# A new hand-out of engines and turn numbers for a two-layer linear-attention and gated-MLP kernel

## The chip, the cores and the metric

The kernel runs on one core of one Trainium2 chip. A core has five engines that run their own instruction streams and meet only at semaphores: TensorE (PE: matmuls, with its weight loads shown apart as PEld), VectorE (DVE), ScalarE (ACT), GpSimd (POOL) and SyncE (SP, which here only issues DMAs). The metric is the device time of one execution in microseconds. Before the change it is 391.01 us, the median of 3 runs (390.86 to 391.19).

## The reference

Input x has 2048 rows of 512 in bf16. Two blocks A and B are applied in turn, twice, each on the layer-normed x and added to x:

```python
x = x + A(layernorm(x)); x = x + B(layernorm(x))      # layer 0
x = x + A(layernorm(x)); x = x + B(layernorm(x))      # layer 1, same weights

# A: linear attention, H = 32 heads of Dh = 16, no mask
q, k, v = split(x @ wqkv)
phi(u)  = concat(softmax(u @ w_phi), softmax(-(u @ w_phi)))    # 32 features a head
kv = phi(k)^T v;  z = sum over rows of phi(k)
o  = (phi(q) kv) / (phi(q) z + 1e-6);  A = o @ wo

# B: gated MLP, F = 1376
B = (relu(x @ W_gate) * (x @ W_up)) @ W_down
```

`kv` and `z` are sums over all 2048 rows, so no query of a layer can be answered before the last key of that layer is in.

## The kernel before

**Tiling.** The rows are 16 tiles of 128, in five slabs of 2, 4, 4, 4 and 2 tiles (`SLABS`). All of x stays on chip. `w_phi` is folded into the key and query weights at the start (`fold`: transposes `wtr`, evictions `wtcp`, products `wcomp`, evictions `wccp`). For every slab and layer there are stages, each with a tag: layer norm (`la`, `lg`), keys and values (`k`), queries (`q`), sums of the query softmax (`z`, `at`), spreading of the denominators (`sp`), numerators (`nm`), output projection (`wo`), gate and up products (`gx`, `gl`) and the down projection (`d`). `gl13` is layer 1, slab 3.

**Layer norm and its transpose.** DVE takes statistics (L844, L869), ACT the root (L871, L873), DVE, ACT or POOL applies it (`ytile`, L886 or L889). The result must be transposed before TensorE can use it: for most slabs by a DMA with transpose that SP issues, one a tile (`ytx`, L894), for the others by TensorE (L918, and the evictions at L817/L820).

**Keys** (`keys`, from L929). A tile has four matmuls for k and four for v (L706), two exponentials of k on ACT (`expk`, L946), their group sums (`Zk`, L952, DVE, 128x1024 to 128x64), the reciprocals (`rZk`: L955 on DVE, or a logarithm and an exponential on ACT, L958 and L959), an eviction of v (`vsb`, L817 on DVE or L820 on ACT), and two products v times 1/Z (`vhat`, L966, on POOL or DVE). Then come the key-value products (`kv`, L978): 32 matmuls of 34 columns a tile, issued for two tiles at a time in slabs of four. They are the shortest matmuls of the kernel.

**An alternative for `Zk`** exists in the code (`sums_by_pe`): two transposing DMAs of `expk` from SP, then eight matmuls of 8 columns on TensorE. The kernel before uses it for no tile.

**Queries** (`queries`, `attend`, from L1037): matmuls with `Wqp`, exponentials on ACT, then sums by short matmuls (`zz`, `zd`, L1062; `za`, L1075), some of which travel through DRAM and back (`zao`, `zai`). Denominators are spread over partitions for slabs 0 and 1 by TensorE (L1184) and multiplied in by DVE (L1202, or after a copy by ACT at L1199), for the other slabs by DMAs (`aTo`, `abT`) and a multiplication on DVE or POOL (L1169). Numerators are L1136, their eviction `oT`.

**The MLP** (`rest`, `glu`) is most of TensorE's work: long runs of 256- and 512-column matmuls (L706), a ReLU on ACT (L1258), a product on DVE (L1260), the down projection and its residual on DVE (L1206).

**What sets the order.** Nothing is ordered by hand. The program makes a list of 3220 operations, each bound to an engine. `ENG` is a dictionary that overrides the default engine of single operations: the key `vh/0/12/1` is the second `vhat` product of tile 12 in layer 0, `vc` an eviction of v, `rz` a reciprocal, `es` and `em` multiplications by the spread denominators, `ap` the application of a layer norm, `yc` the eviction of a transpose, `ot` that of a numerator, `za` that of the sums, `ft` and `fc` evictions of the fold, `ms` memsets and masks, `ld` a load, and `zk` the way in which `Zk` is made. `TURNS` gives each operation a number, in the order in which the program creates them. `schedule()` walks through the list with a small model of the core: of the operations that can start first on an engine, the one with the lowest number goes. The order that comes out, engine by engine, is what the chip executes; each engine is strictly in order and waits on semaphores. The model's constants have no other effect on the program. One part of the model concerns instruction loading: TensorE's stream is cut into pieces of `CHUNK` instructions (two a matmul; the first piece has `CHUNK0`), and a piece may not be entered sooner than `FETCH` nanoseconds after the one before it.

**Fillers.** 18 matmuls with no use of their results (`filler`, L790) carry the number 99999 and run where TensorE would idle early in the program.

In `emit`, an operation that waits on two semaphores gets a separate wait instruction for one of them:

```python
for s, c in self.waits[o.idx]:
    if isinstance(s, int):
        eng.wait_ge(dsems[s], 16 * c)
    else:
        eng.wait_ge(sems[s], c)
ins = o.fn(eng)
```

Of the kernel before, what the change touches and what calls it, by code (L numbers as in the profile page):

```python
# [32 lines left out]
 'ap/a11/2': 'pool',  # L33
 'ap/a11/3': 'act',
 'ap/a12/0': 'act',
 'ap/a12/1': 'pool',
 'ap/a12/2': 'act',
# [3 lines left out]
 'ap/g01/3': 'act',  # L41
# [3 lines left out]
 'ap/g03/1': 'act',  # L45
 'ap/g11/0': 'act',
 'ap/g12/0': 'act',
 'ap/g12/3': 'act',
 'ap/g13/0': 'act',
 'ap/g14/0': 'act',  # L50
# [6 lines left out]
 'em/10/03': 'dve',  # L57
 'em/11/02': 'act',
 'em/11/03': 'dve',
 'es/02/0': 'pool',  # L60
 'es/02/1': 'pool',
 'es/02/3': 'pool',
# [3 lines left out]
 'es/12/1': 'pool',  # L66
 'es/13/0': 'pool',
 'es/13/2': 'pool',
 'es/13/3': 'pool',
 'es/14/2': 'pool',  # L70
 'fck1': 'act',
 'fck3': 'act',
 'fcq2': 'dve',
 'ftk3': 'act',
 'ld/wphi': 'sp',
 'ld/x0': 'act',
 'ms/ZD 0': 'pool',
 'ms/kvs 0 1': 'pool',
 'ms/kvs eps 0': 'pool',
 'ot/00/0': 'dve',  # L80
 'ot/00/1': 'act',
 'ot/00/3': 'act',
 'ot/01/3': 'dve',
 'ot/02/0': 'dve',
 'ot/02/1': 'dve',
 'ot/02/2': 'dve',
 'ot/02/3': 'dve',
 'ot/03/0': 'dve',
 'ot/04/2': 'dve',
 'ot/10/2': 'dve',  # L90
 'ot/11/0': 'dve',
 'ot/11/2': 'dve',
 'ot/12/2': 'dve',
 'ot/13/0': 'dve',
 'ot/14/1': 'dve',
 'ot/14/2': 'dve',
 'ot/14/3': 'dve',
 'rz/0/1': 'act',
 'rz/0/13': 'act',
# [6 lines left out]
 'rz/0/9': 'act',  # L106
 'rz/1/0': 'act',
 'rz/1/10': 'act',
 'rz/1/13': 'act',
 'rz/1/15': 'act',  # L110
 'rz/1/4': 'act',
 'rz/1/6': 'act',
 'rz/1/7': 'act',
 'rz/1/8': 'act',
 'vc/0/2': 'dve',
 'vc/0/5': 'dve',
 'vc/0/6': 'dve',
 'vc/0/7': 'dve',
 'vc/0/8': 'dve',
 'vc/0/9': 'dve',  # L120
 'vc/1/10': 'dve',
 'vc/1/11': 'dve',
 'vc/1/12': 'dve',
 'vc/1/14': 'dve',
 'vc/1/2': 'dve',
 'vc/1/4': 'dve',
 'vc/1/6': 'dve',
 'vc/1/9': 'dve',
 'vh/0/12/1': 'dve',
# [5 lines left out]
 'vh/0/2/0': 'dve',  # L135
 'vh/0/4/1': 'dve',
 'vh/0/7/1': 'dve',
 'vh/0/8/1': 'dve',
 'vh/0/9/1': 'dve',
 'vh/1/1/0': 'dve',  # L140
 'vh/1/1/1': 'dve',
 'vh/1/13/1': 'dve',
 'vh/1/14/1': 'dve',
 'vh/1/15/0': 'dve',
 'vh/1/15/1': 'dve',
 'vh/1/3/0': 'dve',
 'vh/1/3/1': 'dve',
 'vh/1/6/1': 'dve',
 'xp/a02': 'pe',
# [3 lines left out]
 'yc/a00/1': 'dve',  # L153
# [13 lines left out]
 'yc/g00/0': 'dve',  # L167
# [12 lines left out]
 'za/02': 'dve',  # L180
 'za/11': 'dve',
 'za/12': 'dve'}
# [7 lines left out]
-29 100 315 38 249 -1 -5 378 124 183 441 1025 890 766 504 639 1282 1154 1343 1406 1595 1469 1532 1217 1091 1917 150 -100 169 96 147 0 235 48 49 22 51  # L190
70 113 155 198 244 284 326 380 99999 99999 99999 99999 99999 99999 99999 99999 99 84 64 175 296 389 413 -83 467 471 478 484 584 765 770 776 782 825
369 377 433 423 459 724 717 738 744 779 659 665 671 676 701 880 886 891 897 967 544 560 571 572 635 858 863 869 874 903 99999 99999 99999 99999 99999
99999 99999 99999 99999 99999 247 374 -117 444 476 247 589 616 622 628 683 311 393 422 323 492 549 555 577 583 649 799 1078 1099 1271 934 970 1035
1056 1494 1398 1651 1884 1158 1931 2050 828 1143 1164 1183 948 992 1013 1121 1350 1254 1470 1684 2279 1209 2300 2418 3183 3208 3287 1450 1482 1596
1623 1700 1362 1366 1378 1373 1494 1307 1318 1324 1324 1406 1290 1302 1302 1307 1444 595 752 537 653 694 817 759 858 888 957 989 1036 1023 996 1043
1086 1214 1380 1341 1307 1300 1606 1629 1672 1686 1650 1886 1928 1954 1778 1878 1948 2338 2415 2055 3024 2525 1553 1723 1749 1769 1461 1574 1780 1864
1817 1923 2209 2469 2183 2733 2626 1430 1488 1510 1531 1847 1915 1965 2003 1685 1540 2540 2699 2229 2838 3080 1807 2106 2152 2191 2482 2527 2527 2565
2503 2700 2738 2988 3257 2631 3295 3401 3135 4011 4098 924 1029 866 982 1075 1575 1133 1641 1684 1739 1943 1936 1938 2032 2108 1965 2171 2253 2430
2361 2396 2337 2706 2798 2846 2956 2970 3078 3103 3237 3028 3092 3177 3478 3515 3413 3749 3643 2496 2818 2867 2898 2621 2677 2735 2742 3209 3000 3320
3468 3498 2861 3537 3864 2784 3011 3013 3257 3284 3303 3298 3368 3369 3321 3547 3832 3479 4110 3918 2905 2930 3036 3068 3347 3390 3411 3433 3273 3417  # L200
3714 3903 3968 3655 4096 4636 3961 4756 4917 1191 1935 1191 1763 1844 2490 1765 2333 2671 2790 2836 2980 2864 3144 2946 3265 3003 3384 3078 3671 3692
3735 3757 3584 3578 3627 3649 3807 3863 3990 4133 3919 4202 4308 3541 3563 3843 3930 3714 3800 3822 4265 3984 4032 4175 4301 4346 4634 4418 4113 4203
4201 4200 4286 4360 4589 4630 4275 4250 4469 4595 4646 4733 5017 3455 3476 3779 3908 3498 3519 4277 4394 4115 4141 4361 4722 4803 4722 4950 4952 4706
5131 5276 2125 2621 2689 2802 2848 3156 3527 1583 2330 2400 2481 2686 2732 2817 4437 4459 4481 4502 3865 3902 4524 4837 4552 4600 4700 4832 4879 4886
5144 5080 4070 4092 4221 4308 4632 4653 4675 4924 4394 4442 4809 4941 5150 5006 5143 5268 5326 5326 5408 137 224 153 5458 5501 5512 5537 5502 2301
2314 2334 2347 2343 2383 2378 2381 3627 3536 2035 2033 2046 2049 2132 2189 2205 2216 2447 2583 5106 5262 5546 5604 5653 5673 5705 5743 5811 5954 5878
6014 5895 5974 6167 6334 6388 6438 6516 6491 6509 6504 6637 6723 6788 6834 6915 6464 6522 6658 6680 6702 6783 6863 6915 6968 7001 7035 7112 7118 7123
7129 7162 6957 7136 7023 7065 7134 7140 7146 7151 7195 2581 2601 2642 2696 2809 2846 1815 2059 2097 2133 2357 2292 4203 4329 4416 4945 5102 5054 2412
2413 2430 2454 3579 2542 5181 5283 5567 5651 5696 5740 5761 5857 5976 6047 6107 6066 6380 6426 6509 6142 6470 6260 6318 6323 6591 6659 6728 6776 6659
6766 6831 6874 6918 6968 6853 6939 6982 7069 7290 6745 6961 7004 7090 7230 6810 6868 7026 7004 7091 7350 7589 7524 7604 7408 7582 7466 7597 7715 7782  # L210
7828 7821 7814 7980 7911 8225 7842 8260 8066 8391 7925 7218 7268 7234 7243 7678 7686 8051 8061 8114 8199 8522 7273 7612 7623 7634 7645 7656 7667 7694
7749 7771 7792 7847 7913 7924 7934 7945 7734 7985 7339 7350 7361 7372 7437 7459 7481 7579 7382 7393 7404 7421 7426 7448 7424 7503 7619 7691 7306 7317
7507 7514 7546 7557 7568 7601 7251 7262 7284 7295 7309 7525 7535 7590 8246 8316 7814 7825 7858 7869 7902 7956 7967 7978 7836 7918 7989 8000 8011 8022
8033 8033 8065 8139 8067 8076 8085 8097 8113 8118 8143 8143 7705 7716 7727 7738 7760 7730 7803 7880 8186 8251 8223 8267 8288 8310 8443 8464 8486 8507
8529 8989 9027 9185 8159 8180 8202 8245 8387 8421 8551 8572 8594 8615 8861 8972 9294 9361 9069 9279 9391 9488 9703 9346 9504 9696 9878 10465 10583
10630 10312 11431 11603 12580 12497 10420 10374 10876 10785 10937 12732 13713 12996 14406 14363 14453 14005 10745 10692 11539 11598 14372 14119 14410
14577 11401 14635 14749 20550 20652 20690 4816 4880 5323 5302 5409 5361 4373 4545 4567 4902 5313 4958 4859 4988 5010 5075 5214 5166 4967 5025 5404
5420 5527 5479 5722 5857 5883 6201 6560 6607 6631 6707 6750 6867 6804 7141 7078 7267 7330 7393 7456 7519 7204 7427 7641 8078 7855 8335 8541 8422 8422
8481 8788 8840 8883 8904 9026 9331 9309 9339 9431 9672 8637 8659 8680 8767 8817 10932 11123 10044 10404 10269 9127 9286 9616 9657 8892 9245 9879 11100
10730 11380 10496 10716 10726 10909 10680 10785 10798 11640 11092 10558 11494 8926 8934 8943 8951 8959 9003 9063 9104 9144 9252 8831 9191 9215 9175  # L220
9273 9229 9249 9258 9294 9347 9516 10615 10694 10724 10344 9728 9884 9905 9932 10391 10431 9287 9309 9436 9419 9040 9062 9122 9143 9748 9626 9100 9165
9186 9682 9595 9669 9725 9752 9563 9842 8723 8745 8810 9005 9600 9612 9753 9661 11274 11079 9880 10035 9979 10166 9394 9591 9868 10038 10348 10188
9729 9758 9857 9855 8702 9266 9395 9482 9947 10093 10485 10581 10583 10048 10793 10640 10808 10634 11222 11277 10219 9887 10004 9791 10025 10743 10219
10329 10254 10209 10560 10386 10511 10533 9903 9924 9958 10014 10420 10596 10711 10543 10819 10580 11313 10896 10995 10986 11256 11514 11009 11093
11568 12067 11334 11599 11437 11840 11521 11567 11313 11744 11114 10837 11512 11754 11926 11802 11929 12325 12024 11758 12492 12484 10520 11062 10784
# [87 lines left out]
FUSEZ = ()  # L313
ZALL = ()
LATE = 300.0
TRUNC = 0
LASTCUT = ((0, 256), (256, 512))
# [51 lines left out]
class Program:  # L369
# [4 lines left out]
    DMA_BW = 345.0  # L374
    SWITCH = 95.0
    RING = 5500.0
    CHUNK, CHUNK0 = 256, 193
    FETCH, FETCH0 = 3700.0, 9000.0

    def __init__(self):  # L380
# [1008 lines left out]
```

## Time and profile before

| what | value |
|---|---|
| median of 3 runs | 391.01 us (390.86 to 391.19) |
| the profiled execution's own time | 390.13 us |
| its span, first to last instruction | 388.4 us |
| granted TensorE clock | 1.000 |
| PE busy | 376.3 us (97%), 3785 matmuls and as many weight loads |
| DVE busy | 276.0 us (71%), 563 instructions |
| ACT busy | 191.9 us (49%), 428 instructions |
| POOL busy | 75.7 us (19%), 68 instructions |
| instruction loading of one queue | 30 packets, 0.49 MB |

TensorE's busy time counts matmuls that overlap in its pipeline: a 512-column matmul is shown with 379 ns, but the next one starts about 216 ns after it. So what matters is the distance between starts, and the places where a start is late. The chain of work that ended last is followed back from the end; "issue" in it is time in which the engine waited for nothing that the profile shows. Who ended a wait is inferred from the semaphores' events close to the wait's end.

### The profile page before, as it was taken

The numbers are of one execution on the slowest core, as the hardware profiler recorded it, in microseconds if no ns is written. First come the engines' busy times: TensorE is split into PE (matmuls) and PEld (weight loads), VectorE is DVE, ScalarE is ACT, GpSimd is POOL, SyncE is SP. The second block draws the span as 40 slices with busy tenths as digits, with TensorE's granted clock in tenths as the row PEclk, the third lists the DMA queues.
The fourth block names the chain that finished last, engine by engine and source line by source line (L and its number), as shares of the span: only waits on it lengthen the run. The fifth ranks groups of instructions, "written<-read, shape, count | busy, mean of one in ns | idle before, by whom it ended". The sixth has DMA issues, their size and how long they took to land.

```text
span 388.4 us, 9066 instructions
## 1 busy us (share of the span) xinstructions
PE 376.3 (97%) x3785; PEld 198.1 (51%) x3785; DVE 276.0 (71%) x563; ACT 191.9 (49%) x428; POOL 75.7 (19%) x68
## 2 busy tenths in 40 slices
PE   7999998999999999999999989999999999999996
PEld 4554454574444544444566545466444454544564
DVE  8999988977765667664797888788764567345343
ACT  6999689560453524242534478973353134224211
POOL 1065730060200500020223653003002410000000
PEclk9999999999999999999999999999999999999999
DMA  7995001144504212121003010213534132112002
GB/s 241 241 369 101 9 3 56 53 133 83 137 19 97 54 27 54 16 41 28 15 2 62 2 30 3 84 38 113 110 84 127 30 96 55 30 27 54 15 27 63
DMA packets 56970, 27.46 MB, mean 71 GB/s; under 512 B 39296, under 2 KB 55264, under 8 KB 56928
## 3 DMA queue, kind: packets, MB, share of 16 engines
q1 hardware_dynamic: 56352, 26.37, 26.6%
q8 instruction: 30, 0.49, 0.6%
q10 hardware_dynamic: 576, 0.49, 0.4%
q14 instruction: 12, 0.10, 0.1%
HBM read 14.73 MB, written 4.00 MB: 48 GB/s over the span
## 4 chain that ended last, share of the span: by engine, by line
PE 83%; DVE 11%; DMA 4%; issue 1%; ACT 0%; DVEq 0%
PE pb L706 78%; DVE stats L844 3%; DMA yG<-ytile 2%; PE pb L978 2%; DVE Zk L952 2%; DVE expq L1202 1%; DMA yA<-ytile 1%; PE pb L1136 1%; DMA x_sb<-in_A_x_dram 1%; PE pb L1075 1%; DVE yA L817 1%; DVE ytile L889 1%; PE pb L1062 1%; DVE vsb L817 0%; DVE mv L869 0%
## 5 line engine op out<-in xcount | busy, mean ns | idle before, releaser
L706 PE MATMUL pb<-yG,Wg 128*128 128x512 bf16 (+1 forms) x400 | 97.1, 337 | 0.0
L1258 ACT ACTIVATE gate_sb<-pb 128x512 bf16<-128x512 f32 x80 | 47.1, 596 | 99.0 <-PE pb L706 75.1
L706 PE MATMUL pb<-Wd,hT 128*128 128x512 bf16 (+4 forms) x363 | 95.4, 373 | 0.0
L706 PE MATMUL pb<-yG,Wu 128*128 128x512 bf16 (+1 forms) x400 | 91.8, 336 | 0.0
L1260 DVE TENSOR_TENSOR hT<-gate_sb,pb 128x512 bf16<-128x512 bf16 x80 | 54.0, 684 | 47.1 <-PE pb L706 29.4
L1206 DVE TENSOR_TENSOR x_sb<-x_sb,pb 128x512 bf16<-128x512 bf16 x59 | 39.3, 682 | 32.7 <-PE pb L706 32.4
L706 PEld LDWEIGHTS pb<-yG,Wg 128*128 128x128 bf16 x400 | 38.8, 98 | 32.4 <-issue 0.6
L706 PEld LDWEIGHTS pb<-yG,Wu 128*128 128x128 bf16 x400 | 38.8, 98 | 31.0 <-DVE x_sb L1206 0.4
L706 PEld LDWEIGHTS pb<-Wd,hT 128*128 128x128 bf16 (+1 forms) x363 | 34.9, 98 | 35.4 <-issue 0.6
L966 POOL TENSOR_TENSOR vhat<-vsb,rZk 128x544 bf16<-128x544 bf16 x31 | 33.5, 1101 | 55.7 <-DVE rZk L955 18.6
L1169 POOL TENSOR_TENSOR expq<-expq,abT 128x1024 bf16<-128x1024 bf16 (+1 forms) x11 | 20.7, 1899 | 118.1 <-DMA abT<-spread 61.6
L844 DVE BATCH_NORM_STATS2 stats<-x_sb 128x6 f32<-128x512 bf16 x60 | 39.5, 684 | 0.5 <-DMA x_sb<-in_A_x_dram 0.2
L706 PE MATMUL pb<-wv,yA 128*128 128x512 bf16 x128 | 38.0, 379 | 1.5 <-issue 1.5
L706 PE MATMUL pb<-Wkp,yA 128*128 128x512 bf16 x128 | 37.6, 379 | 1.0 <-DMA yA<-ytile 0.8
L706 PE MATMUL pb<-yA,Wqp 128*128 128x512 bf16 (+1 forms) x160 | 34.5, 338 | 0.9 <-DVE Zk L952 0.7
L1047 ACT ACTIVATE expq<-pb 128x512 bf16<-128x512 f32 x64 | 34.4, 613 | 1.7 <-PE pb L706 1.5
L706 PE MATMUL pb<-wo_sb,oT 128*128 128x512 bf16 x128 | 34.6, 379 | 0.0
L946 ACT ACTIVATE expk<-pb 128x512 bf16<-128x512 f32 x40 | 21.9, 612 | 10.0 <-PE pb L706 8.8
L952 DVE TENSOR_REDUCE Zk<-expk 128x64 f32<-128x1024 bf16 x20 | 24.2, 1209 | 1.4 <-ACT expk L946 1.2
L706 PEld LDWEIGHTS pb<-yA,Wqp 128*128 128x128 bf16 x160 | 14.6, 98 | 14.6 <-issue 1.9
L886 ACT ACTIVATE ytile<-x_sb,nmr,rstd 128x512 bf16<-128x512 bf16 x27 | 20.9, 807 | 0.5 <-DVE nmr L878 0.4
L706 PEld LDWEIGHTS pb<-Wkp,yA 128*128 128x128 bf16 x128 | 12.2, 98 | 15.9 <-issue 1.8
(106 smaller groups left out, 374.5 us busy)
## 6 DMA issues: line engine op xcount, KB each, us to landing
abT<-spread SPq DMA_DIRECT2D x32, 128.0 KB
out_dram<-x_sb SPq DMA_DIRECT2D x15, 128.0 KB, 1.8
x_sb<-in_A_x_dram SPq DMA_DIRECT2D x3, 512.0 KB
Wu<-in_B_W_up_dram SPq DMA_DIRECT2D x1, 1280.0 KB, 8.7
Wd<-in_B_W_down_dram SPq DMA_DIRECT2D x1, 1280.0 KB
Wg<-in_B_W_gate_dram SPq DMA_DIRECT2D x1, 1280.0 KB
sums_scr<-abT SPq DMA_DIRECT2D x5, 256.0 KB, 2.7
Zs<-sums_scr SPq DMA_DIRECT2D x5, 256.0 KB, 2.7
```

What stands on the lines that cost most here:

```text
L706: op("pe", lambda e: e.matmul(view(ps), lhsT, rhs, start=start, stop=stop), reads=reads, writes=[ps], occ=max(25.0, 0.4167 * n + 2.6), lat ...
L844: op("dve", lambda e: e.bn_stats(stats[:, t, :], src()), reads=[res], writes=[R("st", t)], occ=580, lat=680, name=f"bn{t}")
L886: op("act", (lambda t, yb: lambda e: e.activation(ytile[:, yb, :], x_sb[:, t, :], ACT.Identity, bias=nmr[:, t, :], scale=rstd[:, t, :]))(t ...
L946: op("act", (lambda i, s, pk: lambda e: e.activation(expk(i)[:, s, :], full(pk), ACT.Exp, scale=1.0 - 2.0 * s))(i, s, pk), reads=[pk], wri ...
L952: op("dve", (lambda i, zb: lambda e: e.tensor_reduce(Zk[:, zb, :], expk(i).rearrange("p s (h f) -> p (s h) f", f=16), AX.X, ALU.add))(i, z ...
L966: op(eng, (lambda i, s, vb, rz: lambda e: e.tensor_tensor(vhat(i)[:, s], vsb[:, vb, :, :], rZk[:, rz, s * 32:(s + 1) * 32].unsqueeze(2).to ...
L978: ins = e.matmul(ps.f32()[32 * i:32 * i + 32, g * 34:g * 34 + 34], expk(tiles[j])[:, sg, f0:f0 + 32], vhat(tiles[j])[:, sg, 8 * c + 2 * i: ...
L1047: op("act", (lambda c0, s, ps: lambda e: e.activation(eqv(st)[:, c0:c0 + per, s, :], ps.f32()[:, 0:per * n].rearrange("p (c n) -> p c n", ...
L1169: op(eng, lambda e: e.tensor_tensor(part, part, abT[:, c].rearrange("p (s n) -> p s n", s=2)[:, :, 0:n], ALU.mult), reads=Re + [R("abT", c ...
L1206: op("dve", lambda e: e.tensor_tensor(x_sb[:, t, :], x_sb[:, t, :], full(ps), ALU.add), reads=[R("x", t), ps], writes=[R("x", t)], occ=597 ...
L1258: op("act", (lambda gb, pg, k: lambda e: e.activation(gate_sb[:, gb, 0:k], pg.f32()[:, 0:k], ACT.Relu))(gb, pg, k), reads=[pg], writes=[R( ...
L1260: op("dve", (lambda gb, hb, pu, k: lambda e: e.tensor_tensor(hT[:, hb, 0:k], gate_sb[:, gb, 0:k], pu.f32()[:, 0:k], ALU.mult))(gb, hb, pu, k),
```

## The change

Three things are replaced and nothing else in the code:

- `TURNS` has 3222 new numbers in place of 3220.
- `ENG` differs in 101 keys. By kind, with what moves:
  - `vhat` (`vh`): 20 products come to DVE and 10 leave it; POOL has 10 fewer.
  - evictions of v (`vc`): 10 leave DVE for ACT, 3 come to DVE.
  - reciprocals (`rz`): 4 leave ACT for DVE, 3 the other way.
  - `zk/9` is new: the sums of tile 9 in layer 0 go by `sums_by_pe`, so DVE loses one `Zk`, SP gets two transposing DMAs and TensorE eight matmuls.
  - layer norm applications (`ap`): 6 come to ACT and 6 leave it; one moves between DVE and POOL each way.
  - `oT` evictions (`ot`): 7 come to DVE and 7 leave it; `za/03` comes to DVE; `em/10/03` goes to ACT with one more eviction.
  - `es`: 5 come to POOL, 5 leave it. Fold: `ftk2`, `fck2` come to DVE; `BD` goes to POOL. `yc/a00/1` and `yc/g00/0` leave DVE. A few memsets change places. `ld/x0` goes from the ACT queue to SP's.
- Of the model's constants, `CHUNK` is 253.6 in place of 256 and `LOADLATE` 150 and 200 ns in place of 100 and 150. `LATE=300` is the value that it had.

Since the numbers set the order, the whole order is new. The key-value products show it. Their turn numbers, first and second group of a slab:

| products | before | after |
|---|---|---|
| layer 0, slab 1 | 3135, 4011 | 3525, 3575 |
| layer 0, slab 2 | 3961, 4756 | 4322, 4801 |
| layer 0, slab 3 | 4706, 5131 | 4877, 5226 |
| layer 1, slab 0 | 20550, 20652 | 19364, 19436 |
| layer 1, slab 1 | 21691, 21741 | 19386, 19811 |
| layer 1, slab 2 | 21791, 22801 | 22019, 22716 |
| layer 1, slab 3 | 22851, 23191 | 22766, 23137 |
| layer 1, slab 4 | 23241, 23288 | 23379, 23426 |

Other numbers that the text below uses: the two DMAs of `zk/9` have 3619 and 3750 and its matmuls 4023; the transposes by DMA of slab 3, layer 0 (`la03`, tiles 12, 11, 13, 10) have 3095, 3226, 3357 and 3488, those of slab 4 (`la04`) 3881 and 4012.

```diff
 ENG = {...
- 'ld/x0': 'act',
+ 'fck2': 'dve',
+ 'ftk2': 'dve',
+ 'ms/BD': 'pool',
+ 'ot/00/2': 'dve',
+ 'za/03': 'dve',
- 'em/10/03': 'dve',
- 'vc/0/6': 'dve',
- 'vc/0/7': 'dve',
+ 'vc/0/11': 'dve',
- 'vc/0/9': 'dve',
+ 'vh/0/10/0': 'dve',
+ 'vh/0/11/0': 'dve',
+ 'vh/0/12/0': 'dve',
- 'vh/0/12/1': 'dve',
...
+ 'zk/9': 'pe'}
 TURNS = """
--29 100 315 38 249 -1 -5 378 124 183 441 1025 890 766 504 639 1282 1154 1343 1406 1595 1469 1532 1217 1091 1917 150
...
+63 50 315 0 252 126 0 441 189 378 504 960 829 698 567 1023 1924 2210 1798 2273 1280 1217 1861 1355 1154 1735 100
...
-ZALL=((0,2),(0,3),(0,4),(1,1),(1,2),(1,3),(1,4)); LASTCUT=((0,384),(384,512)); FILL=(8,10); LOADLATE=(100,150)
+ZALL=((0,2),(0,3),(0,4),(1,1),(1,2),(1,3),(1,4)); LASTCUT=((0,384),(384,512)); FILL=(8,10); LATE=300; LOADLATE=(150,200)
...
-    CHUNK, CHUNK0 = 256, 193
+    CHUNK, CHUNK0 = 253.6, 193
```

## The prediction

> **What bounds the kernel now.** The page first: TensorE is busy 97% of the span, and the chain that ended last lies on it for 83%.
>
> ```profile
> PE 376.3 (97%) x3785; PEld 198.1 (51%) x3785; DVE 276.0 (71%) x563; ACT 191.9 (49%) x428; POOL 75.7 (19%) x68
> PE 83%; DVE 11%; DMA 4%; issue 1%; ACT 0%; DVEq 0%
> q8 instruction: 30, 0.49, 0.6%
> ```
>
> The matmuls themselves change by eight, so the time can move only where a matmul starts late. The waits of TensorE name these places:
>
> ```profile
> PE pb L706 <- issue: 1.5, 1, 1.5
> PE pb L706 <- DMA yG<-ytile: 1.5, 2, 0.8
> PE pb L706 <- DMA yA<-ytile: 0.8, 1, 0.8
> PE pb L706 <- DVE Zk L952: 0.7, 1, 0.7
> PE pb L1062 <- issue: 0.6, 1, 0.6
> ```
>
> Then the timeline of PE around three of them (start, length, what, idle time before it and its releaser):
>
> ```profile
> 43.77 1.24 PE L706 MATMUL pb<-Wkp,yA 128*128 128x512 bf16 x5
> 45.74 0.39 PE L706 MATMUL pb<-yA,Wqp 128*128 128x512 bf16 x1 [0.73 <-DVE Zk L952]
> ...
> 223.66 0.38 PE L706 MATMUL pb<-Wkp,yA 128*128 128x512 bf16 x1
> 225.51 0.38 PE L706 MATMUL pb<-wv,yA 128*128 128x512 bf16 x1 [1.47 <-issue]
> ...
> 241.40 0.38 PE L1062 MATMUL pb<-expq,ZD 128*32 128x64 bf16 x26
> 242.34 0.23 PE L1062 MATMUL pb<-expq,ZD 128*32 128x64 bf16 x6 [0.56 <-issue]
> ```
>
> The third stall cuts one operation of 32 matmuls in two, where no semaphore stands: the instructions were not there. Counted in the trace (weight loads, matmuls and TensorE's separate waits), the last instruction before each gap is number 1217, 4801 and 5569, which is 193 + 256 times 4, 18 and 21. So all three stand at ends of pieces of 256 instructions; 0.49 MB in 30 packets is 16 KB a packet for 7,639 instructions, 255 each. The name that the profile gives to the first (DVE Zk) is then only what happened to end close by: in the program that matmul waits on DVE for kvsum (L988), which ended at 44.14. TensorE had crossed into the piece before at 42.42, 222.02 and 238.88 and goes on at 45.74, 225.51 and 242.34: a piece comes no sooner than 3.3 to 3.5 us after the last crossing. In these stretches 256 instructions were used up sooner, since the key-value products (L978) need about 9 ns a matmul against 216 for a 512-column one; ahead of 223 stand 192 of them in a row. Measured from start to start, less a normal distance, the stalls cost 0.90, 1.63 and 0.74: 3.3 us.
>
> The other places are transposes by DMA that the chain shows to be long:
>
> ```profile
> 32.73 4.47 DMA yA<-ytile
> ...
> 85.96 4.84 DMA yG<-ytile
> ...
> 274.79 3.67 DMA yG<-ytile
> ```
>
> From issue to landing such a transpose takes 2.5 us at the median (this line's answer: 2.4/2.5/4.3). TensorE stood 1.0, 0.87 and 0.92 us for these three. In each, a packet of an instruction queue was being moved (at 35.1, 86.3 and 275.8). Smaller waits are on DVE: about 1.6 us in all at 62.9 to 67.8, where VectorE multiplies spread denominators, and 0.35 at 255.4. The first 9 us are loads and warming.
>
> **The change part by part.** The profiled execution took 390.13 us with its span of 388.4; the median of the runs is 391.01, 0.9 above. I count on the span and put the difference on the median.
>
> *Key-value runs are pulled apart: -3.3 us.* In the old order layer 1's slab 1 (both groups) and the first group of slab 2 have neighbouring numbers (21691, 21741, 21791): the 192 matmuls. In the new one they are 19386, 19811 and 22019, with long matmuls between. In layer 0, 3961 and 4011 (128 matmuls) become 4322 and 3575. The sums that were cut at 242 have moved behind eight more query matmuls. Walking along the sorted new numbers with 193 + 256 n, less as many separate waits as the trace has up to there and with the fillers used in the first 16 us, and pricing by the trace (216 ns, 110 ns, 9 ns), the closest two crossings are 3.8 us apart (between the second group of slab 3 and `zd` of layer 0), the next 4.1 to 4.2 (layer 1, slab 3). Both are above 3.5, so no stall is left: from both sides 0 and -3.3. If the count is off by some 30 instructions, the sums `zd` of layer 1 come 2.8 us after the crossing before: 0.7 is lost again. I take -3.3.
>
> *`zk/9` by TensorE: +0.5.* Eight matmuls; a 128x128 product (`wcomp`) starts 56 ns after the one before, a weight load is 98: 0.45 to 0.8 us, all on the path. Zk's 1.21 us on DVE are saved beside it. The two DMAs occupy SP 1.27 us each, between slab 3's last transpose and slab 4's two, which wait behind them; the wait of the eight matmuls holds every matmul that follows, k and v of slabs 3 and 4. From the DMA number 3750 to 4023, and from 3881 to 4204 (first use of tile 14), about 2.7 to 3.2 us are left against 2.5 needed, so I take no wait; the lost cover is a rival below.
>
> *Late transposes: 0.* The new order again has its shortest leads in the same three places (2.9 to 3.3 us for a transpose of `la03`, `lg01` and `lg11`), each within 2 us of a crossing, and a new one in `la13`. Bounds: -2.8 if all three come free, +1.8 for two new ones at 0.9.
>
> *VectorE's order in the three stages that follow it: +1.3.* At the start `ftk2` and `fck2` (0.31 and 0.60 by neighbouring rows) come into DVE's queue before the layer norms; `BD` (0.59) and a copy (0.33) leave it; but tile 0's load goes second on SP, 0.45 after the first. The chain lies on DVE from 3.9 to 32.7, so I take +0.5 (between -0.5 and +1.5). At 62 to 68 a 256-column `oT` (0.42) and a 512-column copy `za/03` (0.69) join the queue that TensorE waits for: 0 to +1.1, I take +0.4. At 250, `em/10/03` gives DVE 0.26 us back but adds a link over ACT (0.60): -0.3 to +1.0, I take +0.4.
>
> *Hidden.* Engines stay under TensorE:
>
> ```profile
> L966 POOL TENSOR_TENSOR vhat<-vsb,rZk 128x544 bf16<-128x544 bf16 x31 | 33.5, 1101 | 55.7 <-DVE rZk L955 18.6 <-DVE mv L869 17.8 <-ACT rZk L959 8.5
> L966 DVE TENSOR_TENSOR vhat<-vsb,rZk 128x544 bf16<-128x544 bf16 x9 | 6.7, 777 | 0.0
> L817 DVE CAST vsb<-pb 128x512 bf16<-128x512 f32 x14 | 9.5, 684 | 4.1 <-PE pb L706 4.1
> ```
>
> Ten `vhat` cost DVE +7.8 and POOL -11; seven v evictions move 4.8 from DVE to ACT (604 ns each there); with Zk and one more reciprocal (0.55) DVE gains about 2 us in 276. Moves that even out (`ot`, `ap`, `es`) are nothing while those products run under the MLP's matmuls; uncovered, each costs its row, 0.4 to 0.8 us. The model's constants never reach the chip.
>
> Sum: -3.3 + 0.5 + 0 + 1.3 = -1.5 on 388.4: a span of 386.9, and 391.0 - 1.5 = **389.5 us**.
>
> [...]
>
> **Rivals.**
> - *The stalls are only moved.* The count of separate waits and fillers ahead of a place decides where a piece ends, and it is new. Against it: 3.8 us where 3.5 are needed. For it: that is thin, and three places are near. With one to three stalls of 0.7 to 1.6 back: 390.4 to 391.5. The change would then not do what it is said to do.
> - *The three gaps are not loading.* They belong to whatever else ends there (DVE, as the profile says of one), and stay: 391.0 + 1.8 = 392.8. Against it: three of three at the same rest of 256. [...]
> - *SyncE's queue at 34 to 44 us: slower.* Slab 3's transposes, `zk/9`'s two and slab 4's stand in one row, 1.27 us each, with a crossing near 36. A transpose as long as the chain's 4.5 us delays the sums of tile 9 and the transposes behind them; TensorE, in order, stands up to 1 us each for slab 3, the eight matmuls, and slab 4: +3, so 392.5. It decides if more than 2.3 us are lost there (391.8). For it: 1.0 is lost for slab 3 now, without the extra two.
> - *Fewer late transposes.* If two of the three come free, 389.5 - 1.8 = 387.7.
>
> **How the numbers follow.** A measurement can tell about 0.2% (0.8 us) from no change: faster is under 390.2, slower above 391.8. Forecast 0.55 (its own range 388.4 to 390.5, from the small terms); stalls moved 0.17; not loading 0.06; SyncE's queue 0.12; fewer late transposes 0.10. Faster: 0.50 + 0.03 + 0.09 = 0.62; slower: 0.01 + 0.02 + 0.06 + 0.11 = 0.20; same 0.18. The range from 387.7 to 392.3 leaves out the lower half of the last case and the upper parts of the third and fourth.
>
> **What the profile after would show.** No idle time of PE with "issue" over 0.3 us after the first 10 us, and none inside an operation; the word Zk gone from PE's waits. Starts late by 0.7 us or more for yA and yG, three of them. At 40 us eight short matmuls with little idle before them; if more than 0.5, the SyncE rival. 62 to 68 with 1.6 to 2.1 us idle. DVE 277 to 279, POOL 64 to 66 us busy. Gaps that cut a run at 193 + 256 n would make the first term wrong; new waits on DVE or ACT above 1 us elsewhere would make the sum wrong.

## The result, and the profile after

The changed kernel took 388.64 us (median of six runs, 388.32 to 389.36) against 390.94 beside it: a ratio of 0.9938, 95% interval 0.9921 to 0.9956. Forecast were 389.5 against 391.0, a ratio of 0.996, and a range of 387.7 to 392.3. The profiled execution took 388.32 us with a span of 386.5: 1.9 less span than before, where 1.5 were forecast. The size came out nearly as forecast; the working below it did not. The page of the changed kernel:

```profile
PE 371.2 (96%) x3743; PEld 197.6 (51%) x3793; DVE 277.8 (72%) x566; ACT 196.1 (51%) x433; POOL 66.5 (17%) x59
PE 86%; ACT 5%; DVE 3%; DMA 2%; issue 2%; SPq 1%; DVEq 0%; ACTq 0%
q8 instruction: 30, 0.49, 0.6%
```

(PE has 50 matmul records fewer than weight loads: those are missing in the trace, so starts are read from the weight loads below.) TensorE still carries the chain. Its waits (in total, times, longest), lines of the changed kernel being three higher:

```profile
PE pb L709 <- issue: 3.9, 16, 1.5
PE pb L709 <- ACT vsb L823: 0.8, 2, 0.6
PE pb L709 <- ACT oT L823: 0.5, 1, 0.5
PE pb L709 <- DVE stats L847: 0.2, 1, 0.2
```

The names Zk, yA and yG are gone from the long waits, and the gap inside L1062 (now L1065) is gone. But one wait of 1.5 us on "issue" stands there again. The chain of waits shows its place (start, length, what):

```profile
25.07 0.61 PE pb L981 x64
...
28.38 0.71 PE pb L709 x4
29.09 1.48 issue
30.57 8.15 PE pb L709 x38
...
44.01 0.24 issue
44.24 0.34 PE pb L1007 x8
...
87.65 3.22 DMA yG<-ytile
```

The 1.48 us stand between two query products of one group, 256 instructions behind the piece's end at 25.1 (instruction 193 + 512). Measured from weight load to weight load, less the normal distance, it costs 1.65. The eight matmuls of `zk/9` are the L1007 line: 0.34 us, with a late start before them.

Where TensorE lost time, in us, from the starts of all weight loads less normal distances:

| place | before | after |
|---|---|---|
| start of the kernel up to 20 us, the first matmul's later start with it | 3.5 | 4.1 |
| ends of pieces: 44.4, 223.7, 241.6 before; 28.8 after | 1.11 + 1.63 + 0.77 | 1.65 |
| late transposes: slab 3, layer 0; 90 us; 277 us | 1.18 + 1.08 + 1.13 | 0 + 0.31 + 0.84 |
| before the eight matmuls of `zk/9` | - | 0.58 |
| 62 to 75 us | 2.42 | 2.16 |
| 240 to 260 us, the stall at 241.6 set apart | 2.15 | 2.67 |

Two numbers about the ruler, since the effects are below 1%. In the three later groups of runs (the experiments) the kernel before had 389.2 to 389.5 us, with single executions from 387.8 to 392.5; and the changed kernel, run in the second of them once more as `e6_after_again`, gave 0.9981 [0.9960, 1.0002]. So the change is worth 0.2 to 0.6%, depending on the group, and the later interval just includes no change.

### The profile page after: what moved, and what is told of

The parts are those of the page before. It is cut to its first block, busy times and chain, and to the rows that moved or that the text cites. A ratio compares the mean times of both kernels' runs of the same rounds, so it can differ in the third digit from the quotient of the medians.

```text
span 386.5 us, 9068 instructions
## 1 busy us (share of the span) xinstructions
PE 371.2 (96%) x3743; PEld 197.6 (51%) x3793; DVE 277.8 (72%) x566; ACT 196.1 (51%) x433; POOL 66.5 (17%) x59
## 4 chain that ended last, share of the span: by engine, by line
PE 86%; ACT 5%; DVE 3%; DMA 2%; issue 2%; SPq 1%; DVEq 0%; ACTq 0%
PE pb L709 82%; ACT expq L1050 2%; PE pb L981 2%; DMA hT<-in_A_wqkv_dram 1%; PE pb L1139 1%; DMA yG<-ytile 1%; DVE x_sb L1209 1%; ACT vsb L823 1%; ACT abT L823 1%; DVE stats L847 0%; PE pb L1078 0%; ACT expk L949 0%; ACT ytile L889 0%; SPq L732 0%; DVE hT L1263 0%
## 5 line engine op out<-in xcount | busy, mean ns | idle before, releaser
L709 PE MATMUL pb<-Wd,hT 128*128 128x512 bf16 (+3 forms) x353 | 93.1, 372 | 0.9 <-issue 0.6
L709 PE MATMUL pb<-yG,Wu 128*128 128x512 bf16 (+1 forms) x393 | 92.8, 336 | 0.8 <-DVE yG L820 0.3
L709 PE MATMUL pb<-yG,Wg 128*128 128x512 bf16 (+1 forms) x393 | 91.8, 336 | 0.4 <-issue 0.2
L969 POOL TENSOR_TENSOR vhat<-vsb,rZk 128x544 bf16<-128x544 bf16 x26 | 28.1, 1101 | 107.8 <-ACT vsb L823 58.6
L709 PE MATMUL pb<-Wkp,yA 128*128 128x512 bf16 x122 | 36.3, 379 | 1.1 <-ACT vsb L823 0.6
L709 PE MATMUL pb<-yA,Wqp 128*128 128x512 bf16 (+1 forms) x150 | 32.8, 334 | 2.9 <-issue 2.4
L955 DVE TENSOR_REDUCE Zk<-expk 128x64 f32<-128x1024 bf16 x19 | 22.7, 1201 | 5.8 <-ACT expk L949 5.7
L709 PE MATMUL pb<-Wl,yG 128*128 128x192 bf16 x128 | 20.1, 246 | 0.4 <-DVE stats L847 0.2
```

The costliest lines, as they stand in the source:

```text
L709: op("pe", lambda e: e.matmul(view(ps), lhsT, rhs, start=start, stop=stop), reads=reads, writes=[ps], occ=max(25.0, 0.4167 * n + 2.6), lat ...
L955: op("dve", (lambda i, zb: lambda e: e.tensor_reduce(Zk[:, zb, :], expk(i).rearrange("p s (h f) -> p (s h) f", f=16), AX.X, ALU.add))(i, z ...
L969: op(eng, (lambda i, s, vb, rz: lambda e: e.tensor_tensor(vhat(i)[:, s], vsb[:, vb, :, :], rZk[:, rz, s * 32:(s + 1) * 32].unsqueeze(2).to ...
```

## The experiments

Twelve kernels in three groups. Each ratio is to the kernel before run in the same group (389.49, 389.33 and 389.24 us).

| run | group | us | ratio [95%] | profiled span |
|---|---|---|---|---|
| `e1_before_less` | 1 | 386.90 | 0.9927 [0.9905, 0.9950] | 385.9 |
| `e2_after_less` | 1 | 388.16 | 0.9951 [0.9924, 0.9977] | 384.6 |
| `e3_after_more` | 1 | 391.93 | 1.0043 [1.0013, 1.0072] | 389.8 |
| `e5_after_late_w` | 1 | 400.31 | 1.0277 [1.0234, 1.0319] | 399.6 |
| `e6_after_again` | 2 | 388.68 | 0.9981 [0.9960, 1.0002] | 389.5 |
| `e4_after_dve9` | 2 | 389.32 | 0.9999 [0.9979, 1.0020] | 387.5 |
| `e7_before_less_moved` | 2 | 386.08 | 0.9912 [0.9884, 0.9939] | 383.9 |
| `e8_after_less_dve9` | 2 | 388.59 | 0.9972 [0.9954, 0.9990] | 387.5 |
| `e9_after_two_late` | 3 | 388.83 | 0.9978 [0.9964, 0.9993] | 388.1 |
| `e10_after_less_two_late` | 3 | 388.95 | 0.9994 [0.9977, 1.0011] | 387.7 |
| `e11_before_again` | 3 | 389.26 | 0.9997 [0.9981, 1.0014] | 388.1 |
| `e12_before_less_moved2` | 3 | 386.27 | 0.9915 [0.9896, 0.9934] | 384.2 |

### Are the gaps the loading of instructions? Shift the ends of the pieces

The order of every engine is kept. Only the filling matmuls, which compute nothing that is used, are made fewer or more, so that each end of 256 instructions falls on another matmul for the rest of the kernel.

```diff
+PIECES = (((512,), (), (512,), (), (512,), (), (512,), ()), ((), (), (), (), (), (), (), (), (), ()))
-                op("pe", (lambda ps: lambda e: e.matmul(ps.f32()[:, 0:256], ones[:, 0:128], src, start=True, stop=True))(ps),
+                def fill_by(e, ps=ps, widths=PIECES[k][i]):
...
+                    for w in widths:
+                        ins = e.matmul(ps.f32()[:, at:at + w], ones[:, 0:128], (ones if k == 0 else Wkp[:, 0])[:, at:at + w], start=True, stop=True, skip_group_check=True)
```

An empty entry of `PIECES` leaves a filler out. The tuple shown is that of the kernel before with 28 instructions fewer. Three of the fillers left out stood at 75 us, so the ends of pieces fall 22 instructions later up to there and 28 later behind it.

> The kernel before with its order kept; of its 18 filling matmuls of 256 columns at the start, the first eight become four of 512 columns and the other ten are left out (28 instructions fewer by 20 us; the result is the same). Theory, gaps are the loading of instruction runs: every end of a run of 256 falls 28 instructions later in the program, so the three stalls of 1.1 us (44.4), 1.6 us (223.7) and 0.8 us (241.6) go, and at most 0.3 us comes back at one place: 2.5 to 3.0 us less than the kernel before on the span. The instruction packets move about 3 us later too, so that the three late transposes (1.2, 1.1 and 1.1 us) may also go: 1 to 2 us more off. Rival, the gaps are no loading but belong to those products: they stay at the same matmuls with the same lengths, and the time is that of the kernel before within 0.5 us.

At their old places all three gaps are gone; a part of the third stands where its piece now ends. The waits and the chain of this kernel:

```profile
PE pb L716 <- issue: 1.6, 10, 0.2
```

```profile
43.43 4.49 PE pb L716 x20
...
221.57 4.72 PE pb L716 x24
...
238.61 0.35 PE pb L1078 x32
238.96 0.43 PE pb L1091 x7
239.39 0.15 issue
239.54 0.39 PE pb L1091
```

Where 1.47 us stood between products of v and k, 24 matmuls run without a gap, and the 32 sums that were cut (now L1078) run through. But the eight `za` matmuls behind them are cut after seven, at instruction 193 + 256 times 21 again. The chain shows 0.15 us there, because the ends of matmuls are modelled; from the first of the eight weight loads to the product behind them it is 1.10 us, where the same eight take 0.58 in the kernel before. So 0.5 us of the third stall is left, a little more than the 0.3 allowed for, and it has moved with the end of the piece, as the theory has it. The rival (the gaps belong to the products) is out: the same products in the same order run through. In time it is 2.6 us less than the kernel before, on the span of the one profiled execution 2.5. The further 1 to 2 us from transposes did not come: one at 274 us was now late by 1.8.

> The changed kernel with its order kept; the first eight filling matmuls become four of 512 columns and eight of the other ten are left out (24 instructions fewer by 16 us; the result is the same). Loading theory: the end of a run that stood 1.65 us between two query products at 28.8 us moves 24 instructions later, its neighbours are long enough, no stall is left: 1.6 us less than the changed kernel (1.1 at least), about 387.0 us. Rival, that gap belongs to the query products: it stays at 1.5 to 1.7 us at the same matmul, and the time is that of the changed kernel within 0.5 us.

In the profile the gap is gone (27 products in a row where the changed kernel broke after 4), and the span of 384.6 is 1.9 below the changed kernel's:

```profile
27.78 0.66 PE pb L937 x64
...
28.59 5.54 PE pb L719 x27
```

In time a gain is not shown: the median is 388.16 where about 387.0 was expected, its ratio of 0.9951 lies between the changed kernel's own two (0.9938 and 0.9981), and the changed kernel did not run in this group. Three executions of ten took 386.5 to 387.1 and the others 388.1 to 389.1; the profiled one was the lowest.

> The changed kernel with its order kept; twelve of the filling matmuls of 256 columns are each split in two of 128 (24 instructions more, the same TensorE time; the result is the same). Loading theory: the ends of the runs fall 24 instructions earlier; the stall at 28 us grows from 1.65 to about 2.4 us, and new ones come at 59 us (1.1) and at 201 us (1.8): 3.8 us more than the changed kernel, 392 us. Rival, no loading: nothing new, the changed kernel's time within 0.5 us.

The time is the one expected, 391.93 us (0.4% above the kernel before, where the changed kernel's two ratios are below it), but by luck, since the parts agree only in half:

```profile
27.90 0.60 PE pb L937 x57
28.50 1.48 issue
29.98 0.22 PE pb L937 x7
...
60.47 0.22 PE pb L997 x31
60.70 1.04 issue
61.74 0.18 PE pb L997
```

The new stall at 60 us is there, before the last of 32 equal matmuls (1.32 us from load to load, 1.1 were said). The first stayed at 1.66 in place of 2.4. The third, at 201, did not come: the packet for that piece began to move at 196.35, 4.1 us before TensorE reached the piece's end at 200.42, where at the old stalls it began 0.5 to 1.2 us behind the crossing. So the fetch can run ahead of the matmuls (why it does so here is not shown), and counting ends of pieces alone overstates the stalls. A part of the loss that had not been forecast, about 1.7 us, is the clock, granted at 0.50 for 3.4 us (last section).

### Why the stall at 28.8: loading under the weight loads

A crossing is the moment at which TensorE passes the end of a piece. At the old stalls TensorE went on 3.3 to 3.5 us after the last crossing. At 25.1 it took 5.45. Weight loads run there: 246 to 365 GB/s move from 24 to 28 us and 40 from 31 on.

> The changed kernel with the order of every engine kept, but the three large weight loads Wu, Wg, Wd (3.9 MB) issued on SyncE's queue behind the two DMAs of zk/9 (about 41 us) in place of before 25 us; they are first needed near 85 us. Theory, a run of instructions loads more slowly while the weight loads keep the DMA engines busy (5.4 us after the crossing in place of 3.5): the stall of 1.65 us at 28.8 us shrinks to at most 0.3 us, and because the loads now run from 42 to about 56 us, a new stall of 1.0 to 1.5 us comes in the dense stretch at 50 to 59 us, where runs of 256 instructions last 3.8 to 5.2 us. Rival, the early runs load slowly for another reason (their place in the program): the stall at 28.8 us stays at 1.3 us or more and none comes at 50 to 59 us. The total is between 1.7 us less and 2 us more than the changed kernel's: transposes and spread DMAs near 42 to 56 us share the engines with the loads.

The diff takes the three `dma(BIG, ...)` calls from the start to a place behind the two DMAs of tile 9, with `reads=[R("ek", i, 0), R("ek", i, 1)]` added; the order that `schedule()` had found is kept as a list, `ORDER`.

```profile
28.80 8.79 PE pb L701 x42
...
43.21 12.73 DMA yA<-ytile
```

The stall at 29 is gone. The kernel lost 12 us elsewhere, far more than the 2 allowed for: slab 4's transposes are under way together with the loads (319 GB/s from 43 to 56 us), 12.73 us for one in place of 2.5. Because TensorE stood still, no piece ended between 44 and 56, and the second half of the expectation was not tested. So two loads alone were put where nothing follows them on SyncE until 63 us. In `ORDER`, operations 21 (`Wu`) and 22 (`Wd`) move from before 25 us to right behind 458, the last transpose of slab 4, at about 45.5 us:

```diff
+ORDER = """
...
+... 407 458 21 22 353 ...
```

> The changed kernel with every engine's order kept, but two of the large weight loads (Wu and Wd, 2.6 MB) issued behind the last transposes of layer 0's norm (about 45.5 us) in place of before 25 us; SyncE has nothing else to issue until 63 us. Theory, the instruction packet waits while weight loads occupy the DMA engines: the loads in front now end near 22 to 24 us, the packet starts at most 1.2 us after the crossing at 25 us and the stall of 1.2 to 2.0 us near 29 us shrinks to 0.3 us or less; the loads run from 46 to 55 us instead, so that the packets after the crossings at 45.6 and 50.8 us may start up to 3 us late and a stall of 0 to 1.4 us may come near 51 or 55 us. In sum 0.3 to 2 us less than the changed kernel. Rival: the stall near 29 us stays above 1 us.

The stall moved with the loads. In the chain:

```profile
28.89 8.79 PE pb L701 x42
...
51.35 0.26 PE pb L1057 x29
51.61 1.54 issue
53.15 0.23 PE pb L1057 x3
```

At 29 it runs through; at 51.6, with the loads now running, 32 equal matmuls are cut after 29 (1.74 us from load to load, a little above the 1.4 said). In the changed kernel the same operation at 52.4 has no gap. The packet behind the crossing at 46.15 started 4.6 us late here, with 377 GB/s under way from 48 to 50 us; behind the same crossing in the changed kernel it was 1.2 us, with 8 GB/s. With all else in the same order, this shows the cause from both sides: a piece comes later while weight loads move. In sum nothing was gained (388.83, where 0.3 to 2 us less had been expected).

> The same with the 24 instructions fewer at the start (as in the first group), so that the second and third ends of runs stand 5.8 us apart. If the spread of the earlier kernel with 24 fewer (386.5 to 389.1 us) came from the packet that waited for the weight loads in some executions, the slower group goes: median 386.3 to 387.3 us. Rival, its spread has another cause: median above 387.8 us as before.

The median was 388.95, so the expectation failed: the two late loads again put a stall at 52 (1.45 us), and the spread stayed.

```profile
52.05 0.10 PE pb L989 x7
52.15 1.25 issue
53.40 0.60 PE pb L989 x57
```

So the spread of e2 is not settled by this run. What it may be is seen in `e8` below.

The readings of that early piece in the kernels of the changed order, from the DMA records of the trace (the 16 KB instruction packet that starts next):

| kernel | crossing | packet starts | TensorE goes on | after crossing |
|---|---|---|---|---|
| changed | 25.12 | 27.93 | 30.57, stalled | 5.45 |
| e3 | 25.38 | 27.23 | 29.98, stalled | 4.60 |
| e4 | 25.77 | 27.75 | 30.76, stalled | 4.99 |
| e6 | 25.85 | 28.83 | 31.66, stalled | 5.81 |
| e8 | 26.07 | 30.09 | 33.03, stalled | 6.96 |
| e2 | 25.40 | 28.53 | 31.19, no stall | at most 5.79 |
| e9, loads away | 25.63 | 25.00 | 29.32, no stall | at most 3.69 |
| e5, loads away | 25.54 | 25.04 | 29.24, no stall | at most 3.70 |
| e10, loads away | 26.02 | 27.06 | 31.78, no stall | at most 5.76 |

With the loads the packet starts 1.9 to 4.0 us behind the crossing; without them (under 30 GB/s from 24 to 28 us) it starts 0.5 and 0.6 ahead of it or 1.0 behind. TensorE goes on 1.3 to 1.6 us after the packet's end everywhere it stalled. With the loads the delay differs by 2 us among kernels whose orders are nearly the same; between the two executions of the changed kernel itself (the row "changed" and e6) it differs by 0.2. Bulk loads are not the only thing beside which a packet is late: in the changed kernel those behind the crossings at 64.9 and 108.6 start 4.0 and 4.5 us late, with 70 and 112 GB/s of other transfers under way. TensorE does not stall there, since its next 256 instructions take 9.8 and 22.2 us.

### One part undone: tile 9's sums by VectorE again

> The changed kernel with one part undone, its order kept: the sums of tile 9 in layer 0 come from a VectorE reduction again (before Zk11's), the two transposing DMAs are gone, and eight matmuls on constants stand in TensorE's stream where the eight products stood, so that no run of instructions ends elsewhere. Forecast's term: TensorE pays 0.35 us for the eight in both, the late start of 0.6 us before them at 43.4 us goes: 0.4 to 0.7 us less than the changed kernel. Rival: the reduction's 1.1 us on VectorE makes vhat of tiles 9 to 13 late, a wait of 0.3 us or more comes before the key-value products at 44 to 47 us in its place, and the time is the changed kernel's within 0.3 us.

```profile
PE pb L701 <- issue: 3.1, 14, 1.0
PE pb L975 <- DVE vhat L963: 0.7, 1, 0.7
```

The late start before the eight is gone, and the rival's wait is there, later than it said: the key-value products of slab 3 (L975) wait for `vhat` at 52.3, 0.93 us from load to load. The time is 0.6 us above the changed kernel's in the same group, within the intervals of both, where 0.4 to 0.7 less had been forecast. So in time no difference is shown: `zk/9` on TensorE costs about what it saves.

> The changed kernel with 24 instructions fewer at the start and the sums of tile 9 by VectorE: if the stall at 28.8 us and the late start before tile 9's products add up, 1.65 + 0.5 us less than the changed kernel beside it, that is 0.5 to 0.6 % less. Rival, the gain of the stall is given back to TensorE's later waits for VectorE (62 to 68 us, 250 us) and to late transposes, because TensorE comes to them 1.65 us earlier: less than 0.8 us in all.

388.59, 0.1 us less than the changed kernel where 0.5 to 0.6% were forecast: the sum did not come. In the profiled execution the packet started 4.0 us late, and the stall stood at the piece's end that e2 had passed without one:

```profile
29.25 2.96 PE pb L711 x15
32.21 0.81 issue
33.03 2.12 PE pb L711 x9
```

The same shift of 24 instructions is thus enough in e2's profiled execution and not in e8's (1.19 us lost from load to load here). If e2's own executions differ in the same way, that would give its spread of 2 us. That is argued, not shown: the two kernels differ in tile 9's sums, and only one execution of each is profiled.

### The two kernels once more

> The changed kernel as it is, beside the others of this group: 386.5 us of span in the profile, the stall of 1.6 to 1.7 us after the crossing at 25.1 us, and 0.4 to 0.8 % less than the kernel before. If late transposes differ from execution to execution, the losses near 90 and 277 us differ from the 0.3 and 0.8 us seen first.

The stall was 2.0 us, tile 9's late start 0.51, the transposes at 280 us 1.23, and a new loss came behind the stall (the clock, last section). The profiled execution was the slowest of the twelve (391.23 us), and its span of 389.5 is longer than that of the kernel before in its second profile (388.1); so this second pair can speak for single terms, not for the sum.

> The kernel before as it is, for a second profile beside the others: the three stalls at 44.4, 223.7 and 241.6 us stand again (1.0 to 1.2, 1.5 to 1.8 and 0.7 to 0.9 us), since no weight load runs there; the late transposes may differ.

The three stalls stand as before, 0.95, 1.63 and 1.04 us from load to load. The chain:

```profile
44.98 0.58 issue
...
223.88 1.47 issue
...
241.31 0.31 PE pb L1062 x26
241.62 0.83 issue
```

TensorE went on 3.2, 3.5 and 3.7 us after the crossing before, so the 3.3 to 3.5 of the first profile is no sharp limit. The transposes cost 0.74, 1.11 and 0.72 in this one, 2.57 against 3.39 in the first.

### Late transposes, and a kernel below both

Kernel e1 had its largest remaining loss in a transpose (issued 271.6, landed 275.96) and an instruction packet that moved from 273.6 to 274.8. In the next two, matmuls that need no transpose are drawn in front of those that do.

```diff
-... 2400 2401 2402 2403 2404 2405 2376 2377 2367 2368 ...
+... 2376 2377 2367 2368 2372 2373 2378 2400 2401 2402 2403 2404 2405 ...
```

> The kernel before with 28 instructions fewer at the start (as in the first group) and three moves in TensorE's order: seven attention output matmuls (wo9, wo7, wo8 of slab 2, layer 1) before the gated stage's first matmuls that wait for transposes at 274 us, three (wo8, layer 0) before those at 88 us, two (k11) before k13 at 36 us. Theory, the late transposes cost the end what TensorE stands there (1.8, 0.4 and 0.8 us with the 28 fewer): 1.5 + 0.4 + 0.4 us less than without the moves, about 384.5 us. Rival, what is saved there is lost at the next wait, because VectorE and ScalarE are what the later work waits for: at most 0.5 us less than without the moves (386.4 to 386.9 us).

The chain of e1 there, and that of e7:

```profile
271.61 4.35 DMA yG<-ytile
275.96 0.05 issue
276.01 3.11 PE pb L716 x21
```

```profile
271.05 1.40 PE pb L708 x6
272.46 0.05 issue
272.51 6.66 PE pb L708 x40
```

The 1.8 us are gone, and the span fell by 2.0 (2.3 were said). The two profiled executions flatter this: e1's was the second slowest of its ten (387.65), e7's the fastest of its six (385.64). By the medians, 386.90 and 386.08 in two groups, it is 0.8 us; the intervals of the two ratios overlap, and the forecast of 384.5 was missed. Against the kernel before e7 is 0.9%, against the changed kernel in the same group, 386.08 to 388.68, 0.7% less. This version beats both. The move at 88 us gave nothing: that place waited on `oT` by VectorE, 0.5 us as before. How much of the 1.8 the moved matmuls cover isn't told apart, because the packet also came 3.3 us behind that transpose's issue in place of 2.0: it took 2.52 us, and the next two took 4.14 and 3.26.

> The kernel before with 28 instructions fewer and moves in TensorE's order: the seven attention output matmuls at 274 us and the two of k11 at 36 us as in the second group, without the three of wo8 at 88 us, and six query products (q0, q1) before k15, which waits for a transpose at 228 us. If late transposes cost what TensorE stands, 0.5 to 0.7 us less than the kernel with the first three moves: 385.3 to 385.7 us, about 0.9 to 1.1 % less than the kernel before. Rival: what is saved at 228 us returns at the attention stage behind it; the time of the kernel with the first three moves.

The late start at 228 us is gone, but the time is e7's, as the rival said (386.27 against 386.08, ratios 0.9915 and 0.9912): 0.75 us were late again at 276, where a transpose took 4.25. What was saved at one transpose is no more than what the same transposes differ by between two executions of the kernel before (0.8 us in all).

## Why the prediction came out right, and where it was wrong

By the forecast's own terms, first forecast, then measured on the two first profiles:

- *Key-value runs are pulled apart*: -3.3; measured -3.5 + 1.65 = -1.9 (from weight load to weight load the old three are 3.5). That the gaps are loading is shown (e1, e3, e9), and the three went. The step that failed is "so no stall is left": I priced every crossing by the 3.5 us of the three old stalls, and none of those had weight loads beside it (5, 40 and 5 GB/s from the crossing before to where TensorE went on, against 246 to 365 in the changed kernel from 24 to 28 us). My walk found its closest two crossings where they came out (56.6 and 60.4, 3.8 apart, no stall), but it did not name those at 25.1 and 28.8: they are 3.7 apart, above 3.5 and below the 5.45 that the piece took there. The trace before already held the delay: behind its crossing at 24.04 the packet started at 27.75, 3.7 us late, and nothing stalled only because the next crossing came at 33.2. The gap at 193 + 256 n, which the forecast had named as the sign against this term, is there. The rival "the stalls are only moved" was half true, for another reason than its own.
- *`zk/9` by TensorE*: +0.5; measured 0.35 + 0.58 = +0.9. The step that failed is "so I take no wait": I reckoned 2.5 us for the two DMAs, but a packet moved from 40.34 to 41.85 and they took 4.13 and 3.60. The rival of SyncE's queue named this and priced it at 3; it was 0.6, just over the 0.5 that the forecast had set as that rival's sign.
- *Late transposes*: 0; measured -2.2 (3.39 to 1.15; in the second pair of profiles 2.57 to 1.23, so -1.3). The step that failed is that leads of the same length give the same loss. For slab 3 it goes with whether a packet moves while the transpose is under way: its late one took 4.47 us beside one before, and its four met none in the changed kernel and took 2.41 to 2.48. At 90 and 277 us this does not explain it: packets moved there in the changed kernel too (88.41 and 275.23) and the late transposes took 3.2 to 4.2 us, yet TensorE stood less; why is not shown. The rival "fewer late transposes" came true for one place and most of a second.
- *VectorE's order in three stages*: +1.3; measured +0.6 at the start, -0.3 at 62 to 75, +0.5 at 250: about +0.9. Start and the third were sized about right; the second was not there. (Eight short sums have left the window of 62 to 75; for equal work, 59.4 to 69.5 us before and 60.4 to 70.5 after, the second is nearer -0.1.)

Sum of the measured terms -1.9 + 0.9 - 2.2 + 0.9 = -2.3; the span gives -1.9, so 0.4 us more was lost elsewhere (the largest single window, 100 to 210 us, has 0.67 more). Two errors of opposite sign, 1.4 in the first term and 2.2 in the third, nearly cancelled: that the time came out so close is luck, and half of the working was not right. All of this rests on one profiled execution of each kernel.

Over all the runs each stall stands at 193 + 256 n, counted to within one instruction. The stalls came where 256 instructions lasted less than the 3.2 to 3.7 us that a piece took, and under weight loads less than 4.6 to 7.0; e3's crossing at 200.4, behind which 256 instructions lasted 1.5 us with no stall, shows that not every such place has one.

What stays open: which part of the way the packet waits for under the loads (only its late start is seen); why its delay differs among nearly equal kernels, and the transposes between executions; and why the kernel before was 1.5 us slower beside the changed kernel's first runs (390.94) than in the three groups of the experiments.

## What to carry to other kernels

Count TensorE's instructions, and look where 256 of them last less than the 3.2 to 3.7 us that a piece took in these runs, or the 4.6 to 7.0 while bulk loads ran: a stall with "issue" as its releaser that cuts a run of equal matmuls at such a place is probably loading. A shift of a few dozen instructions, by fewer or more idle matmuls, is a cheap test for it and, here, no worse a cure: 28 fewer in the old order gave at least as much as all the new turn numbers (0.993 against 0.994 and 0.998). Look at the distance between weight loads, not at the idle time alone: a stall of 0.5 us showed as 0.15. When only a sum is right, compare term by term before the model is trusted with the next change.

## What the runs showed that I had not expected

- Transposes by DMA took longer with an instruction packet beside them. Over the fourteen profiles, after 60 us: 111 transposes with a 16 KB instruction packet starting within 2.35 us after their issue took 3.75 us at the median, 101 of them over 2.9; 577 with none near took 2.48, 46 over 2.9. In one order shifted by 28 instructions (before and e1) the same transposes change sides: tile 7, layer 1, 4.43 to 2.52 us; tile 13, 4.20 to 2.54; tile 15, which meets a packet at 225.5 in e1, takes 3.86. It is not all: of the slow ones with no such packet near, one at 101 us in the changed kernel took 4.5 us, and what lengthened it is open.
- A stall of 1.84 us in e6 and one of 1.48 in e3 cost more behind them. In e6 the granted clock fell after the stall of 1.84 us ahead of it, and 12 matmuls filled 4 us (columns: window, PE busy and so on, PEclk third from the end); the changed kernel's first profile has no such drop after its 1.48:

```profile
29.82 1.84 issue
31.65 5.50 PE pb L709 x18
```

```profile
31.60:35.60 4.00, 3.95 (x12) 1.60 (x12) 2.07 (x9) 2.70 (x8) 0.80 (x1) 0.57 0.03 7
35.60:38.00 2.40, 2.40 (x13) 1.08 (x11) 1.75 (x4) 1.68 (x4) 0.00 (x0) 1.00 0.27 55
```

  Cut to the drop itself, the granted clock is 0.50 from 31.64 to 35.05 us, so about 1.7 us are lost. In e3 it came after 1.48 us of "issue", again 0.50 for 3.4 us (31.02 to 34.42), and eight of its ten executions show a mean clock of 0.996 or less: these took 391.0 to 392.6 us, the other two 389.5 and 389.6. The clock of 0.50 came after 1.84 us of "issue" in e6 and 1.48 in e3, and not after 1.48 in the changed kernel's first profile; what decides is not shown.
